# Three reorderings in a gated linear-attention plus mixture-of-experts kernel: the queue of the gate-weight loads, the step in which rows are placed, and the place of decay's exponential

## The chip, the cores and the metric

The kernel runs as one program on one core of a Trainium2 chip. The metric is device time in microseconds, lower is better. A core has a matrix engine (TensorE, PE in the rows; PEld is its weight load), a vector engine (VectorE, DVE), a scalar engine (ScalarE, ACT) that evaluates functions from tables, a general engine (GpSimd, POOL) and an engine that mostly starts transfers (SyncE, SP). ACT, POOL and SP each start DMA transfers from queues of their own. An engine takes its instructions in the order in which they were written, so an instruction that waits holds up everything behind it on its engine.

## The reference, cut to what matters

A recurrent attention with a forget gate, then a mixture of experts in which each token goes to one expert and none is dropped.

```python
# q, k, v, f_logit: (4, 8, 768, 48) float32
f = 1.0 / (1.0 + np.exp(-f_logit))
state = np.zeros((B, H, D, D))
for t in range(S):
    state = f[:, :, t, :, None] * state + np.einsum('bhd,bhe->bhde', k[:, :, t], v[:, :, t])
    y[:, :, t] = np.einsum('bhd,bhde->bhe', q[:, :, t], state)
x = y.transpose(0, 2, 1, 3).reshape(3072, 384)
logits = x @ w_gate                                  # 8 experts
expert_idx = np.argmax(logits, axis=1)
gate_w = softmax(logits)[expert_idx]
for e in range(8):                                   # rows of expert e
    y[rows] = np.maximum(x[rows] @ w1[e], 0.0) @ w2[e]   # 384 -> 1024 -> 384
return gate_w[:, None] * y
```

## The kernel before

**Attention, in twelve units.** The sequence is cut into chunks of 128 tokens; a unit `u` is one chunk of two batches and all eight heads (`NU = 12`). A loop over `n` runs fourteen steps, and step `n` works on several units at once: scores of unit `n`, outputs of unit `n - 1`, and the gate logits and row layout of unit `n - 2`, while the decays of units `n + 1` to `n + 3` are prepared ahead. In this text "step n" begins with the first score matmul of unit `n`, and its start is called S.

**What a unit needs.** `growth` takes the exponential of the forget logit on ACT (L363) and adds one on POOL (L364). `product` is a running product along the sequence on DVE (L371, tile `r`). `by_r` multiplies `k` by `r` on POOL (L383). `log_r` (ACT logarithm, L388) and `decay` (ACT exponential, L394) turn `r` into the decay that `by_decay` multiplies into `q` on DVE (L402). The logarithm and the exponential each need a table load on ACT (`ACT_TABLE_LOAD`). `score` multiplies `q` and `k` on PE (L413) into PSUM tiles `s`, and DVE copies the causal part into `at` with predicated copies (L417), four in a step: two behind the first half of the scores and two behind the second. There are three buffers for `s`, so the second half of the scores needs the first predicated copies done.

**The rest of a step on PE.** `keys` transposes `k` (L426, `kp`; ACT copies the result to `kn`, L431), `rows` multiplies the attention output `ys` of unit `n - 2` by a constant matrix `wx` that holds an identity for laying out rows and the gate weights (L521, `xp`), `within` and `before` make the attention output (L439 and L460, `yt`, copied to `ys` by ACT, L501), `added` makes the state's increment (L476, `dp`), and every second step two small matmuls count the rows by expert (L203 and L204, `rp`). The tiles `kp`, `xp`, `dp` and `rp` share three PSUM buffers in rotation (pool `pst`, tag `tr`), two of `kp`, two of `xp`, one of `dp` and one of `rp` in such a step. So the first `xp` of the next step takes the buffer that `rp` had.

**Routing.** Units are taken in pairs. At the end of an odd step n from 3 to 11, `rows` has finished a pair, `choose` has picked experts (DVE, L191 to L199), `count` has made `rp`, and then `place` and `fill` turn ranks into row numbers: nine small DVE instructions (L210 to L237), which sit on DVE between the state update (L493) and the next step's predicated copies. `sends` then scatters rows of 400 floats to DRAM from POOL (L166), half of a group per step.

**Constants and loads.** `load_consts` starts two transfers from ACT's queue, the mask `mpack` (L152) and the packed constants `fpack` (L153), and behind them four small ones that write the gate weights into the columns of `fpack` that `wx` covers (L157). The last four wait until `fpack` has landed, since they write into it. SP's queue carries the loads of `f`, `k`, `q` and `v` (L356), with the next unit's `f` waiting until an old buffer is free, and the clearing of row regions in DRAM (L323).

**Experts.** Behind the attention come eight experts of three tiles of 128 rows, on PE almost without a gap.

The order of the instructions is written out by hand: what the loop calls first stands first on each engine.

Of the kernel before, what the change touches and what calls it, by code (L numbers as in the profile page):

```python
# [10 lines left out]
F32 = mybir.dt.float32  # L11
# [3 lines left out]
OP = mybir.AluOpType  # L15
AX_X = mybir.AxisListType.X
PSUM = bass.MemoryType.PSUM

B, H, S, D = 4, 8, 768, 48
# [93 lines left out]
def kernel(  # L113
# [22 lines left out]
    def const(name):  # L136
        a, w = fat[name]
        return fpack[:, a : a + w]
# [12 lines left out]
    def load_consts():  # L151
        nc.scalar.dma_start(mpack, nc.inline_tensor(mv, name="c_mpack").ap())  # L152
        nc.scalar.dma_start(fpack, nc.inline_tensor(fv, name="c_fpack").ap())  # L153

        for a, r in halves:
            for b, cols in enumerate((slice(XW, WX), slice(0, E))):
                nc.scalar.dma_start(  # L157
                    wx[r, :, cols],
                    moe_w_gate.rearrange("(p two d) e -> two d p e", two=2, d=D)[a ^ b],
                )  # L160
# [168 lines left out]
    with ExitStack() as st:  # L329
# [56 lines left out]
        def log_r(u, part=whole):  # L386
            x = units[u]
            nc.scalar.activation(x["f"][:, part, 1:CR], x["r"][:, part, 1:CR], AF.Ln)  # L388
# [96 lines left out]
        def update(u):  # L485

            x = units[u]
            new = wk.tile([128, SEG, D], F32, name="state", bufs=4)
            last = _bc(x["last"], 2, D)
            if x["old"] is None:  # L490
                nc.vector.tensor_copy(new, x["dp"])
            else:
                nc.vector.tensor_tensor(new, x["dp"], x["old"], op=OP.add)  # L493
            nc.gpsimd.tensor_tensor(new, new, last, op=OP.mult)
            states[u % 2] = new

        def settle(u):
            x = units[u]
# [6 lines left out]
        def rows(u):  # L505
# [3 lines left out]
            if u == g[0]:  # L509
                n = 2 * len(g)  # L510
                group["xr"] = wk.tile([128, n, ROW], F32, tag="xr", name="xr", bufs=3)
                group["lg"] = wk.tile([128, n, E], F32, tag="lg", name="lg")
                b0 = 2 * (u % 2)
                toks = const("tok").rearrange("p (b c) -> p b c", c=NC)[:, b0 : b0 + n, u // 2]
                nc.gpsimd.tensor_copy(group["xr"][:, :, TOK], toks)
                nc.gpsimd.memset(group["xr"][:, :, USED:ROW], 0.0)
            for a in range(2):
                j = 2 * (u - g[0]) + a
                xp = pst.tile([128, HP, XW], F32, name="xp", **tr)
                for p in range(HP):  # L520
# [4 lines left out]
                        start=True,  # L525
                        stop=True,
                    )
                to = group["xr"][:, j, 0:DM].rearrange("p (h w) -> p h w", h=HP)
                if a:
                    for h in range(2):  # L530
                        nc.scalar.copy(
                            to[:, :, D * h : D * h + D],
                            xp[:, :, XW - D * h - D : XW - D * h],
                        )
                else:
                    nc.scalar.copy(to, xp[:, :, 0 : 2 * D])
                gate = slice(0, E) if a else slice(2 * D, XW)
                nc.vector.reduce_sum(  # L538
                    group["lg"][:, j],
                    xp[:, :, gate].rearrange("p h e -> p e h"),  # L540
                    axis=AX_X,
                )
            if u != g[-1]:
                return None
            return Route(wk, group["lg"], lead["base"], group["xr"], "xs")

        st.enter_context(tc.manual_schedule(engines=ordered))
        ab = (slice(0, HP), slice(HP, SEG))
# [29 lines left out]
        def narrow_early(x, w):  # L578
            narrow(x, w, pst.tile([128, DM], F32, name="yp", **tr), None)

        sends = []
        for n in range(NU + 2):
            here, back, last = n, n - 1, n - 2
            rt = None
# [6 lines left out]
            if n + 1 < NU:  # L591
                by_r(n + 1)
                log_r(n + 1)
            if sends:
                sends.pop(0)()
            if here < NU:
# [8 lines left out]
                    rt.choose()  # L605
            if n + 1 < NU:
                decay(n + 1)
            if n + 3 < NU:
                growth(n + 3)
            if rt:  # L610
# [13 lines left out]
                    by_decay(n + 1, part)  # L624
            if here < NU and here // 2 < NC - 1:
                added(here)
                update(here)
            if rt:
                rt.count(pst.tile([128, 2, rt.n, E], F32, name="rp", **tr))
                rt.place()  # L630
                rt.fill()
                lead["base"] = rt.after
                if n == NU - 3:
                    lack = wk.tile([1, EARLY], F32, name="lack", bufs=1)
                    some = wk.tile([1, 1], F32, name="some", bufs=1)
                    nc.vector.tensor_tensor(
                        lack, rt.after[0:1, 0:EARLY], const("full")[0:1, 0:EARLY], op=OP.is_lt
                    )
                    nc.vector.reduce_max(some, lack, axis=AX_X)
                    nc.vector.tensor_copy(fix, some)  # L640
                if n < NU:
                    for c in range(0, rt.n, 2):
                        sends.append(lambda rt=rt, c=c: rt.send(range(c, c + 2)))
                else:
                    rt.send(range(rt.n))
            if n == NU:
                early_h = early_banks()
                widen(soon[0], weights[0], early_h, range(3))
# [3 lines left out]
                load(n + 4, "f")  # L652
            if n + 3 < NU:
                load(n + 3, "kqv")
            if n < 2:
                for e in range(4 * n, 4 * n + 4):
                    load_pads(e)
# [358 lines left out]
```

## Time and profile before

| What | Value |
|---|---|
| Time, median of 3 runs | 464.23 us (461.31 to 464.49) |
| Profiled execution | 462.27 us, of which span 460.4 us from the first to the last instruction |
| PE busy | 412.5 us (90%), 3580 instructions |
| DVE busy | 168.0 us (36%) |
| ACT busy | 123.3 us (27%) |
| POOL busy | 118.2 us (26%) |
| Moved | 98.33 MB, mean 214 GB/s |

The table is an average over two different halves: some 188 us of attention and routing, in which all engines and the DMA share the work, and some 272 us of experts, which is PE's alone. In the rows, an instruction's idle time in brackets is what its engine waited before it, with the releaser. The granted clock is that of TensorE: 1.00 is 2.4 GHz and 0.50 is 1.2 GHz.

### The profile page before, as it was taken

What the parts mean: (1) busy time and instruction counts of PE and PEld (TensorE: products, weight loads), DVE (VectorE), ACT (ScalarE), POOL (GpSimd) and SP (SyncE); (2) the same over time, 40 slices, a digit from 0 to 9 for tenths busy, and PEclk for the clock granted to TensorE, in tenths of its full rate; (3) what the DMA queues carried; (4) which work ended last, traced back from release to release, by engine and by line L of the source; (5) the groups of instructions that cost most, each with busy time, mean ns of one, the idle gap of its engine ahead of it and who ended that gap; (6) DMA issues with size and microseconds to landing.
All of it is one profiled execution on the core that took longest, in us unless ns stands there. A gap on an engine that the chain in (4) does not pass through costs nothing.

```text
span 460.4 us, 8555 instructions
## 1 busy us (share of the span) xinstructions
PE 412.5 (90%) x3580; PEld 333.1 (72%) x3581; DVE 168.0 (36%) x359; ACT 123.3 (27%) x184; POOL 118.2 (26%) x134
## 2 busy tenths in 40 slices
PE   0178979798979998999999999999999999999992
PEld 0167869697869887777778888857588888777460
DVE  4188895959794554111111211122111111211110
ACT  2677867768674320000000000001000000000010
POOL 6257564748573141000000011000100000000000
PEclk9999997979997999999999999999999999999998
DMA  8999983739981224699992451540079999100000
GB/s 287 348 365 390 390 302 129 263 120 366 338 297 55 76 87 145 220 391 381 393 388 98 154 187 36 183 178 1 31 262 392 395 390 389 38 17 19 18 2 21
DMA packets 42862, 98.33 MB, mean 214 GB/s; under 512 B 3856, under 2 KB 27717, under 8 KB 42816
## 3 DMA queue, kind: packets, MB, share of 16 engines
q1 hardware_dynamic: 38496, 87.48, 52.6%
q0 software_dynamic: 3200, 9.64, 5.5%
q8 instruction: 29, 0.48, 0.4%
q10 hardware_dynamic: 1120, 0.59, 0.4%
q14 instruction: 17, 0.14, 0.1%
HBM read 81.46 MB, written 16.63 MB: 213 GB/s over the span
## 4 chain that ended last, share of the span: by engine, by line
PE 78%; DVE 10%; issue 3%; ACT 3%; DMA 3%; POOL 0%; ACTq 0%; POOLq 0%; DVEq 0%
PE hps L268 26%; PE yps L282 25%; PE s L413 5%; PE xp L521 4%; PE yt L439 3%; PE s L268 2%; PE hps L796 2%; PE yps L824 2%; PE yp L282 2%; DMA fpack<-c_fpack 2%; DVE at L417 2%; PE etp L255 2%; DVE place L225 2%; PE kp L426 2%; DVE r L371 2%
## 5 line engine op out<-in xcount | busy, mean ns | idle before, releaser
L268 PEld LDWEIGHTS hps<-xT,w1t 128*128 128x128 f32 x1056 | 121.1, 192 | 7.3 <-issue 2.3
L268 PE MATMUL hps<-xT,w1t 128*128 128x128 f32 x1056 | 121.8, 275 | 0.0
L282 PE MATMUL yps<-w2t,hT 128*128 128x384 f32 x352 | 117.2, 486 | 0.0
L282 PEld LDWEIGHTS yps<-w2t,hT 128*128 128x128 f32 x352 | 65.2, 190 | 40.8
L166 POOL DMA_INDIRECT out_dram<-ysb,dst x26 | 25.3, 971 | 254.8 <-DVE ysb L289 254.8
L276 ACT ACTIVATE hT<-hps 128x512 f32<-128x512 f32 x22 | 13.1, 597 | 220.0 <-PE hps L268 220.0
L413 PE MATMUL s<-q,k 64*128 64x128 f32 x384 | 34.8, 312 | 36.4 <-POOL last L397 21.7
L413 PEld LDWEIGHTS s<-q,k 64*128 64x128 f32 x384 | 28.7, 210 | 40.2 <-POOL last L397 25.4
L278 DVE TENSOR_SCALAR hT<-hps 128x512 f32<-128x512 f32 x22 | 15.2, 691 | 105.9 <-PE hps L268 105.9
L289 DVE TENSOR_SCALAR ysb<-yps,xrow 128x384 f32<-128x384 f32 x22 | 13.6, 618 | 93.3 <-PE yps L282 93.3
L417 DVE COPY_PREDICATED at<-mpack,s 128x512 f32<-128x512 uint8 x48 | 32.2, 724 | 12.5 <-PE s L413 12.5
L166 POOL DMA_INDIRECT xs<-xr,posi x24 | 27.5, 1147 | 22.9 <-DVE lg L538 8.9
L371 DVE TENSOR_TENSOR_SCAN r<-f,cap 128x1032 f32<-128x1032 f32 (+1 forms) x13 | 28.9, 2225 | 2.3 <-POOL f L364 2.1
L521 PE MATMUL xp<-fpack,ys 128*128 128x104 f32 x192 | 29.4, 317 | 0.2 <-ACT ys L501 0.2
L521 PEld LDWEIGHTS xp<-fpack,ys 128*128 128x128 f32 x192 | 27.2, 226 | 1.7 <-issue 0.4
L383 POOL TENSOR_TENSOR k<-k,r 128x1024 f32<-128x1024 f32 (+1 forms) x13 | 27.1, 2086 | 3.4 <-DVE r L371 3.4
L439 PE MATMUL yt<-at,v 128*64 128x128 f32 x384 | 26.8, 299 | 0.0
L439 PEld LDWEIGHTS yt<-at,v 128*64 128x64 f32 x384 | 23.9, 153 | 1.5 <-issue 0.6
L402 DVE TENSOR_TENSOR q<-q,f 128x512 f32<-128x512 f32 x24 | 17.2, 757 | 21.2 <-ACT f L394 21.2
L397 POOL COPY last<-f 128x8 f32<-128x8 f32 (+1 forms) x13 | 9.9, 768 | 46.1 <-ACT f L394 46.1
L388 ACT ACT_TABLE_LOAD x12 | 15.4, 1283 | 10.9 <-issue 10.7
L364 POOL TENSOR_SCALAR f<-f 128x1032 f32<-128x1032 f32 (+1 forms) x13 | 14.7, 1136 | 3.3 <-ACT f L363 3.3
(109 smaller groups left out, 357.3 us busy)
## 6 DMA issues: line engine op xcount, KB each, us to landing
qw<-in_moe_w_dram SPq DMA_DIRECT2D x16, 1536.0 KB, 12.5
w1t<-in_moe_w_dram SPq DMA_DIRECT2D x8, 1536.0 KB, 9.9
w2t<-in_moe_w_dram SPq DMA_DIRECT2D x8, 1536.0 KB, 13.6
xs<-pad SPq DMA_DIRECT2D x8, 800.0 KB, 11.4
v<-in_vu_dram SPq DMA_DIRECT2D x12, 512.0 KB, 5.6
f<-in_fu_dram SPq DMA_DIRECT2D x11, 516.0 KB, 7.0
k<-in_ku_dram SPq DMA_DIRECT2D x11, 512.0 KB, 7.8
q<-in_qu_dram SPq DMA_DIRECT2D x11, 512.0 KB, 4.9
```

The costliest lines, as they stand in the source:

```text
L166: ins = nc.gpsimd.indirect_dma_start(out=dst, out_offset=bass.IndirectOffsetOnAxis(ap=idx, axis=0), in_=src, in_offset=None, bounds_check= ...
L268: nc.tensor.matmul(hp[g][:, f, :], lhsT=w[0][:, j, b * 128 : b * 128 + 128], rhs=x["xT"][:, j, :], start=j == 0, stop=j == KD - 1,)
L278: nc.vector.tensor_scalar(x["hT"][:, 4:8], hp[1], 0.0, None, op0=OP.max)
L282: nc.tensor.matmul(yp, lhsT=x["hT"][:, f, :], rhs=w[1][:, f, :], start=f == 0, stop=f == NF - 1)
L371: nc.vector.tensor_tensor_scan(x["r"][:, part].rearrange("p s c -> p (s c)"), x["f"][:, part].rearrange("p s c -> p (s c)"), cap[:, part]. ...
L383: nc.gpsimd.tensor_tensor(k, k, r[:, :, 1:CR], op=OP.mult)
L388: nc.scalar.activation(x["f"][:, part, 1:CR], x["r"][:, part, 1:CR], AF.Ln)
L402: nc.vector.tensor_tensor(q, q, x["dec"][:, part], op=OP.mult)
L413: nc.tensor.matmul(ps[h][:, p], lhsT=x["k"][r, s], rhs=x["q"][r, s], start=True, stop=True)
L417: nc.vector.copy_predicated(x["at"][:, a, h], _bc(causal, 1, HP), ps[h])
L439: nc.tensor.matmul(x["yt"][DP * (h ^ a) : DP * (h ^ a) + DP, a, p], lhsT=x["v"][:, a, 2 * p + h], rhs=x["at"][:, a, h, p], start=p == 0, s ...
L521: nc.tensor.matmul(xp[:, p], lhsT=x["ys"][:, a, p], rhs=wx[:, p, 0:XW] if a else wx[:, p, E:WX], start=True, stop=True,)
```

## The change

1. The four gate-weight transfers move from ACT's queue at the start to SP's queue, in step 0 behind the loads of that step and ahead of the clearing of row regions (`load_gate`).
2. `place` and `fill`, which stood at the end of a routing step, move into the following step, behind its first score half, `by_r` and `log_r` (function `settled`). On DVE that is behind the step's first two predicated copies. In the last two steps they stay where they were. The POOL multiply of the state (L494) moves with them, behind the next unit's `by_r`, in every step.
3. The ACT copies of the laid-out rows (L531, L536) leave `rows` and become `lay`, behind `decay`. The DVE reduction of the gate logits (L538) stays and so now stands ahead of those copies.

```diff
@@ load_consts
         nc.scalar.dma_start(fpack, nc.inline_tensor(fv, name="c_fpack").ap())
+    def load_gate():
         for a, r in halves:
             for b, cols in enumerate((slice(XW, WX), slice(0, E))):
-                nc.scalar.dma_start(
+                nc.sync.dma_start(
                     wx[r, :, cols],
...
@@ update
-            nc.gpsimd.tensor_tensor(new, new, last, op=OP.mult)
             states[u % 2] = new
+            return lambda: nc.gpsimd.tensor_tensor(new, new, last, op=OP.mult)
@@ rows -> rows, lay
-                to = group["xr"][:, j, 0:DM].rearrange("p (h w) -> p h w", h=HP)
-                if a:
-                    for h in range(2):
-                        nc.scalar.copy(
...
-                else:
-                    nc.scalar.copy(to, xp[:, :, 0 : 2 * D])
                 nc.vector.reduce_sum(
...
+        def lay(u):
+            x = units[u]
+            for a in range(2):
+                to = x["xr"][:, a, 0:DM].rearrange("p (h w) -> p h w", h=HP)
+                if a:
+                    for h in range(2):
+                        nc.scalar.copy(
...
+                else:
+                    nc.scalar.copy(to, x["xp"][a][:, :, 0 : 2 * D])
+        def settled(n, rt):
+            rt.place()
+            rt.fill()
+            lead["base"] = rt.after
...
+            if n < NU:
+                for c in range(0, rt.n, 2):
+                    sends.append(lambda c=c: rt.send(range(c, c + 2)))
+            else:
+                rt.send(range(rt.n))
@@ the loop
             if n + 1 < NU:
                 by_r(n + 1)
                 log_r(n + 1)
+            if later:
+                settled(*later)
+                later = None
+            if decayed:
+                decayed()
+                decayed = None
             if sends:
                 sends.pop(0)()
...
             if n + 1 < NU:
                 decay(n + 1)
+            if 0 <= last:
+                lay(last)
...
-                update(here)
+                decayed = update(here)
             if rt:
                 rt.count(pst.tile([128, 2, rt.n, E], F32, name="rp", **tr))
-                rt.place()
-                rt.fill()
-                lead["base"] = rt.after
...
+                later = (n, rt)
+                if n >= NU:
+                    settled(*later)
+                    later = None
...
+            if n == 0:
+                load_gate()
```

How the instructions stand is shown at three places. First ACT at the start of the program, before, from the first exponential on (`f` is the forget logit, `r` the running product):

```order
L363 ACTIVATE f<-f 128x516 x2
L152 DMA mpack<-c_mpack 128x128
L153 DMA fpack<-c_fpack 128x1075
L157 DMA fpack<-in_moe_w_gate_dram 48x4x8 x4
L388 ACT_TABLE_LOAD
L388 ACTIVATE f<-r 128x4x128 x2
```

and of the change:

```order
L365 ACTIVATE f<-f 128x516 x2
L152 DMA mpack<-c_mpack 128x128
L153 DMA fpack<-c_fpack 128x1075
L390 ACT_TABLE_LOAD
L390 ACTIVATE f<-r 128x4x128 x2
```

The table load for the first logarithm now stands right behind the start of `fpack`; the four transfers stand on SP behind `v` of unit 3. Second DVE from step 3's `by_decay` to step 4's running product, before (`lg`, `oh`, `ex` are logits, choice and exponents, `rp` the counts, `place` and `posi` row numbers, `su` and `xr` the gate weight):

```order
L402 TENSOR_TENSOR q<-q,f 128x512 x2
L493 TENSOR_TENSOR state<-dp,state 128x384
L210 COPY counts<-fpack 128x8
L211 COPY counts<-rp 128x8x4
L212 SCALAR_TENSOR_TENSOR sums<-fpack,counts 128x40
L222 TENSOR_TENSOR place<-rp,sums 128x32
L225 TENSOR_TENSOR place<-place,oh 128x32
L228 TENSOR_REDUCE posi<-place 128x4
L235 TENSOR_REDUCE su<-ex 128x4
L236 TENSOR_SCALAR su<-su 128x4
L237 RECIPROCAL xr<-su 128x4
L417 COPY_PREDICATED at_97<-mpack,s 128x512 x4
```

and of the change:

```order
L404 TENSOR_TENSOR q<-q,f 128x512 x2
L495 TENSOR_TENSOR state<-dp,state 128x384
L419 COPY_PREDICATED at_97<-mpack,s 128x512 x2
L212 COPY counts<-fpack 128x8
L213 COPY counts<-rp 128x8x4
L214 SCALAR_TENSOR_TENSOR sums<-fpack,counts 128x40
L224 TENSOR_TENSOR place<-rp,sums 128x32
L227 TENSOR_TENSOR place<-place,oh 128x32
L230 TENSOR_REDUCE posi<-place 128x4
L237 TENSOR_REDUCE su<-ex 128x4
L238 TENSOR_SCALAR su<-su 128x4
L239 RECIPROCAL xr<-su 128x4
```

The nine small instructions now stand between the first two and the last two predicated copies. Third ACT in a routing step, before:

```order
L431 COPY kn<-kp 128x512 x2
L536 COPY xr<-xp 128x384
L531 COPY xr<-xp 128x4x48 x2
L394 ACT_TABLE_LOAD
L394 ACTIVATE f<-f 128x8x128
L363 ACTIVATE f<-f 128x1032
L231 ACTIVATE ex<-ex 128x32
```

and of the change:

```order
L433 COPY kn<-kp 128x512 x2
L396 ACT_TABLE_LOAD
L396 ACTIVATE f<-f 128x8x128
L554 COPY xr<-xp 128x384
L549 COPY xr<-xp 128x4x48 x2
L365 ACTIVATE f<-f 128x1032
L233 ACTIVATE ex<-ex 128x32
```

The table load and the exponential of `decay` no longer stand behind the three copies that read `xp`; `growth`'s exponential (L365) still does.

## Rows read from the trace of the kernel before

**Rows 1.** Page, part 2: forty slices of 11.5 us, granted clock in tenths.

```profile
PEclk9999997979997999999999999999999999999998
```

**Rows 2.** Stretches, step by step: length, busy us and instructions by engine, clock, DMA.

```profile
60.80:76.10 15.30, 12.82 (x154) 11.65 (x153) 10.58 (x19) 9.02 (x14) 8.11 (x10) 0.78 0.44 163
76.10:85.80 9.70, 9.70 (x162) 8.73 (x158) 8.06 (x17) 8.32 (x13) 7.36 (x7) 1.00 0.79 271
...
110.80:122.90 12.10, 9.62 (x154) 8.53 (x153) 10.07 (x19) 8.12 (x13) 6.77 (x9) 1.00 0.93 364
...
132.60:147.00 14.40, 11.77 (x122) 10.55 (x121) 8.34 (x21) 6.51 (x9) 6.16 (x9) 0.76 0.35 132
147.00:187.90 40.90, 39.52 (x380) 33.42 (x373) 19.80 (x89) 9.09 (x22) 11.38 (x15) 1.00 0.28 96
187.90:460.40 272.50, 262.34 (x1715) 200.21 (x1713) 44.96 (x95) 15.50 (x26) 24.28 (x25) 0.99 0.53 193
```

**Rows 3.** Timeline of the start: start us, length us, engine, instruction [idle before].

```profile
4.58 0.73 ACTq L153 DMA_DIRECT2D fpack<-c_fpack  x1
4.92 2.81 DVE L371 TENSOR_TENSOR_SCAN r<-f,cap 128x516 f32<-128x516 f32 x2 [0.76 <-POOL f L364]
...
13.62 1.87 ACTq L157 DMA_DIRECT2D fpack<-in_moe_w_gate_dram  x4
...
15.51 1.28 ACT L388 ACT_TABLE_LOAD   x1 [10.69 <-issue]
...
20.77 2.08 PE L413 MATMUL s<-q,k 64*128 64x128 f32 x16 [20.77 <-POOL last L397]
...
25.71 1.06 ACT L388 ACTIVATE f<-r 128x1024 f32<-128x1024 f32 x1 [2.09 <-DVE r L371]
...
32.43 2.08 PE L413 MATMUL s<-q,k 64*128 64x128 f32 x16 [2.11 <-DVE q L402]
```

**Rows 4.** DMA issues at 13.98 and at 44.27 us: size, us to landing.

```profile
f<-in_fu_dram SPq DMA_DIRECT2D x1, 516.0 KB, 4.4
...
f<-in_fu_dram SPq DMA_DIRECT2D x1, 516.0 KB, 11.1
```

**Rows 5.** One stretch, 16 to 58 us: columns as in Rows 2.

```profile
16.00:58.00 42.00, 31.67 (x382) 28.62 (x384) 30.85 (x35) 34.63 (x44) 22.84 (x23) 1.00 1.04 381
```

**Rows 6.** Timeline of step 4, behind the routing of step 3.

```profile
61.05 0.55 DVE L210 COPY counts<-fpack 128x8 f32<-128x8 f32 x1
...
62.33 2.17 POOL L383 TENSOR_TENSOR k<-k,r 128x1024 f32<-128x1024 f32 x1
...
62.74 1.80 DVE L225 TENSOR_TENSOR place<-place,oh 128x32 f32<-128x32 f32 x1
...
65.19 1.31 DVE L417 COPY_PREDICATED at<-mpack,s 128x512 f32<-128x512 uint8 x2
...
65.94 1.16 PE L413 MATMUL s<-q,k 64*128 64x128 f32 x14 [2.48 <-DVE at L417]
```

**Rows 7.** Timeline, the same small instructions at 156 us.

```profile
155.83 0.19 DVE L211 COPY counts<-rp 128x32 f32<-128x32 f32 x1 [1.41 <-PE rp L204]
...
156.57 0.19 DVE L225 TENSOR_TENSOR place<-place,oh 128x32 f32<-128x32 f32 x1
```

**Rows 8.** Stretches of 1 us, PE alone: busy, instructions, granted clock, DMA.

```profile
64.00:65.00 1.00, 0.00 (x0) 1.00 0.88 318
67.00:68.00 1.00, 1.00 (x6) 0.50 0.55 217
```

**Rows 9.** Timeline of step 5, which has no placing in it.

```profile
75.25 1.07 ACT L501 COPY ys<-yt 128x512 f32<-128x512 f32 x2 [0.58 <-PE yt L460]
...
77.38 1.36 DVE L417 COPY_PREDICATED at<-mpack,s 128x512 f32<-128x512 uint8 x2 [0.52 <-PE s L413]
...
78.60 1.06 ACT L431 COPY kn<-kp 128x512 f32<-128x512 f32 x2
...
79.39 2.03 PE L521 MATMUL xp<-fpack,ys 128*128 128x104 f32 x16
```

More of the change, by code (lines that the diff above doesn't have):

```diff
@@ L516, in rows @@
                 nc.gpsimd.memset(group["xr"][:, :, USED:ROW], 0.0)
+            x["xr"], x["xp"] = group["xr"][:, 2 * (u - g[0]) :], []
             for a in range(2):
@@ L527, in rows @@
                     )
-                to = group["xr"][:, j, 0:DM].rearrange("p (h w) -> p h w", h=HP)
-                if a:
-                    for h in range(2):
-                        nc.scalar.copy(
-                            to[:, :, D * h : D * h + D],
-                            xp[:, :, XW - D * h - D : XW - D * h],
-                        )
-                else:
-                    nc.scalar.copy(to, xp[:, :, 0 : 2 * D])
                 gate = slice(0, E) if a else slice(2 * D, XW)
@@ L542, in rows @@
                 )
+                x["xp"].append(xp)
             if u != g[-1]:
@@ L545, in rows @@
             return Route(wk, group["lg"], lead["base"], group["xr"], "xs")
+        def lay(u):
[5 more added lines that the diff above has]
+                        nc.scalar.copy(
+                            to[:, :, D * h : D * h + D],
+                            x["xp"][a][:, :, XW - D * h - D : XW - D * h],
+                        )
+                else:
+                    nc.scalar.copy(to, x["xp"][a][:, :, 0 : 2 * D])
         st.enter_context(tc.manual_schedule(engines=ordered))
@@ L579, in narrow_early @@
             narrow(x, w, pst.tile([128, DM], F32, name="yp", **tr), None)
-        sends = []
+        def settled(n, rt):
+            rt.place()
+            rt.fill()
+            lead["base"] = rt.after
+            if n == NU - 3:
+                lack = wk.tile([1, EARLY], F32, name="lack", bufs=1)
+                some = wk.tile([1, 1], F32, name="some", bufs=1)
+                nc.vector.tensor_tensor(
+                    lack, rt.after[0:1, 0:EARLY], const("full")[0:1, 0:EARLY], op=OP.is_lt
+                )
+                nc.vector.reduce_max(some, lack, axis=AX_X)
+                nc.vector.tensor_copy(fix, some)
+            if n < NU:
[3 more added lines that the diff above has]
+                rt.send(range(rt.n))
+        sends, later, decayed = [], None, None
         for n in range(NU + 2):
@@ L626 @@
                 added(here)
-                update(here)
+                decayed = update(here)
             if rt:
                 rt.count(pst.tile([128, 2, rt.n, E], F32, name="rp", **tr))
-                rt.place()
-                rt.fill()
-                lead["base"] = rt.after
[L633 to L645, printed above, removed]
+                later = (n, rt)
+                if n >= NU:
+                    settled(*later)
+                    later = None
             if n == NU:
```

## The prediction

> **What bounds the kernel now.** The stretches come first: the experts take 272.5 of the 460.4 us and PE is busy in 262.3 of them [rows 2]. The change touches nothing there, so they only move earlier. What is left are 188 us of start and attention. Step by step these split into steps without placing, in which PE has no gap (9.70 us, of which 9.70 busy; the other two such steps, 7 and 9, also take 9.7), and steps that follow a routing step and hold its placing: 15.3, 12.1 and 14.4 us for steps 4, 8 and 10, and step 6 is like step 4 [rows 2]. So PE bounds every second step, and something else costs 2.4 to 5.6 us in the others. The timeline of step 4 names it: PE stands still for 2.48 us ahead of the last 14 of 16 instructions of a score group, released by a predicated copy that starts at 65.19, because DVE has been at the nine small instructions since 61.05 [rows 6].
>
> The clock line comes next: most of the span at 9 tenths or more, with a few slices of 7 [rows 1]. In 64 to 65 us PE does nothing; in 67 to 68 it is busy throughout at a granted clock of 0.50, which is 1.2 GHz [rows 8]. Step 8 has the same 2.48 us of idle PE (12.10 less 9.62) at a clock of 1.00 and takes 12.1 us; steps 4 and 6 take 15.3 at a mean clock of 0.78 [rows 2]. So the same wait costs once or twice: itself, and in three of these four steps some 3.2 us more of half clock.
>
> Last the start. ACT starts the transfer of `fpack` at 4.58, for 0.73 us. It then stands for 10.69 us until its table load at 15.51; within that, at 13.62, it takes 1.87 us to start the four gate loads. The running products that the logarithm needs end at 7.73 (4.92 + 2.81). PE's first score is at 20.77, step 1 at 32.43 [rows 3].
>
> **Change 1, the gate loads: about -6.6 us.** Without them the table load follows at 5.31 and is over by 6.6; the second half of the logarithm waits for 7.73. From the table load to the first score it is 5.26 us now (15.51 to 20.77), so the first score comes between 11 and 14, 7 to 9 us earlier. That doesn't all last. ACT meets `growth` of unit 2 next, whose `f` is started at 13.98 and lands 4.4 us later, at 18.4 [rows 4], and I do not expect it much sooner: the DMA engines are full (381 GB/s, share 1.04) from 16 to 58 us [rows 5]. From 18.4 on ACT needs about 1.0 for that exponential and 1.28 for a table load, so the logarithm of unit 1 starts near 20.7 instead of 25.71: -5.0. In the kernel before, that logarithm waited for a running product and the product of unit 2 was late again behind it; with both early, step 1 starts some 1.6 us sooner still, near 25.8 instead of 32.43. I take -6.6. Bounds: -1.9, if only the issue time goes, and -10.7, the whole idle time. On SP the four loads cost 1.87 us of issue and stand ahead of the clearing of row regions and of `f` of unit 5, all behind a DMA that is full anyhow; `wx` is first read in step 2, more than ten us later. I cost that at nothing; without that cover it is 1.9 us.
>
> The Trainium skill ("DMA: Bandwidth & Descriptors", section "Issuing engines are not separate DMA queues") says that all queues run on the same 16 engines and that another issuing engine saves only the issue time, which is usually small. By that rule the change would be worth the 1.87 us of the four issues. The trace differs: the larger part of the 10.69 us is a wait that stood on ACT's queue for `fpack` to land.
>
> **Change 2, the placing: a wait of 2.48 becomes one of about 0.8.** Let S be a step's start. Step 5 shows where things fall without placing (S = 76.18): the first two predicated copies at S + 1.2 for 1.36, so to S + 2.56, and `xp` at S + 3.2 [rows 9]. With the nine instructions behind those two copies, the second score half no longer waits for them. The next to wait is `xp`: its PSUM buffer is the one that held `rp`, and the last reader of `rp` is the fourth of the nine (L222). With POOL quiet, L211 to the end of L222 take under 0.74 us (155.83 to 156.57) [rows 7], so with the first one about 0.9: `rp` is free at S + 3.5 and PE loses about 0.4. With POOL busy, L225 took 1.80 us rather than 0.19 and ended with POOL's L383 (62.33 + 2.17 = 64.50) [rows 6, 7]. L383 now starts earlier, ahead of the state multiply, so most of it should be over by S + 2.6; if the chain still meets all of it, the wait is 0.4 + 2.2 = 2.6. I take 0.8, nearer to the quiet end. The gap itself falls away, and with it, I expect, the half clock: no step that lost less than 2.4 us shows it.
>
> The Trainium skill ("SBUF — State Buffer", section "SBUF: two separate sides") calls this an exclusive lock between DVE and GpSimd, held for a whole instruction. The 1.80 us above agree. It gives no duration that the sum uses.
>
> **Change 3, decay ahead of the copies: no gain by itself, a wait of 0.6.** It takes the three copies (about 1 us) and their wait for `xp` off the way from logarithm to `by_decay`; in a step without a gap (9.70) nothing waits for that. But the copies now wait for the logit reduction on DVE, behind the running product. That reduction ends near S + 8.5 to S + 9.1 in a step with placing (2.56, the nine at about 1.9 to 2.5, then 1.36, 2.3 and 0.3). Behind it ACT has the copies and `growth` (2.0), then `ys` to the first `kn` (75.25 to 79.1, 3.9) [rows 9]: S + 14.4 to S + 15.0. The second `xp` of the next step needs the `kp` buffer that this `kn` copy frees, at S + 9.9 + 4.2 = S + 14.1. So the steps without placing lose 0.3 to 0.9; I take 0.6.
>
> **The sum.** A step with placing has 9.62 busy us in step 8 [rows 2], of which some 0.5 belong to a score group that is cut in two and counted longer; 9.1 remain, and 9.9 with the new wait of 0.8. Step 4 gets 11.1: `f` of unit 6 is started at 44.27 and lands at 55.4 [rows 4], and a step 4 that begins at 54.2 has ACT waiting for it ahead of `ys` and `kn`. I put 2.0 for that and the 0.8 together (0.4 to 3.5).
>
> - Start to step 4: -6.6.
> - Step 4: 15.3 to 11.1, -4.2. Step 6: 15.3 to 9.9, -5.4. Step 8: 12.1 to 9.9, -2.2. Step 10: 14.4; it has the same wait and half clock as step 6, -5.4.
> - Steps 5, 7, 9: 9.7 to 10.3, +1.8 together.
> - From 147.0 on (40.9 and 272.5): no change. The fifth placing, in step 12, has slack there.
>
> Together -22.0. Against the profiled execution's own 462.27 us this is 440.3, so **440 us**; that execution is 0.4% under the median of 464.23, and the runs differ by 3.2 us, about one stretch of half clock.
>
> **Rivals.**
> - *The half clock stays.* The new waits (0.8 and 0.6, 2.0 in step 4) still make it fall in three steps. For it: the start, and step 4 with its late `f`. Against it: each wait is a third of the old one or less, save in step 4. Price 3 x 3.2 = 9.6: 450 us.
> - *The start gives its gain back.* The loads are full until 58 us [rows 5], so step 4 comes only 1.9 us earlier, by issue time alone. This is also the skill's rule above. Against it: a table load and a logarithm that wait for no load. Price 4.7: 445 us.
> - *The placing only moves its wait.* `xp` waits 2.5 us instead of the scores, with the same half clock. Then only the start and the 1.8 remain: 462.3 - 6.6 + 1.8 = 457.5 us.
> - *Slower.* `xp` waits longer than the scores did, because the chain on DVE meets the growth, `by_r` and state instructions of POOL one behind the other. At 4.4 us in each of five steps (+9.6), with two more half clocks (+6.4) and the start's -6.6, it is 472 us. It decides from a wait of about 3.8 us, where 5 x 1.3 eat up the 6.6. Against it: L383 was the only long one in the way in step 4 [rows 6], and 2.6 is its bound.
>
> **How the numbers follow.** About 1% of the time, 4.6 us, is what a measurement of this kernel can tell from no change. Chances: forecast 0.63, within 436 to 445; half clock stays 0.17; start given back 0.08; placing only moves 0.06; slower 0.03; two of these together and no change 0.03. The bounds of the waits (0.4 to 2.6 in three steps, 0.4 to 3.5 in one) are -2.8 and +6.9, those of the start -4.1 and +4.7, and few of them fall together; 434 to 451 takes in the first three cases. Faster 0.94, same 0.03, slower 0.03.
>
> **What the profile after would show.** ACT's first table load for the logarithm at 5 to 7 us, the first score at 11 to 14 and step 1 at 25 to 27; if step 1 is later than 30, the start failed. No idle PE between the two score halves of steps 4, 6, 8 and 10, a short wait ahead of `xp` in its place, and a second one ahead of the second `xp` of steps 5, 7 and 9. A granted clock of 1.00 through the steps from 4 on. Steps of about 10 us and a tail from step 11 on as long as before. Wrong would be a wait of over 2 us ahead of `xp`, or a clock that falls as often as before.

## The result, and the profile after

The changed kernel took **441.33 us** (median of 4 runs, 440.55 to 441.52) against 463.05 us before: a ratio of 0.953 (95% interval 0.949 to 0.957). On a second occasion, beside the last three experiments, it took 438.45 us (438.00 to 439.31) against 461.46, 0.949 (0.946 to 0.953). The forecast was 440 us. The first profiled execution took 440.55 us with a span of 438.7, 21.7 less than the span before; the working had 22.0 less. The total is nearer than its parts deserve, as the steps show.

The clock line of the page, to be read against [rows 1], has no dip left until the program's end:

```profile
PEclk9999999999999999999999999999999999999997
```

For the start the clock that the rows print says nothing, in either kernel: [rows 5] prints 1.00, but 16 score matmuls take 2.08 us there ([rows 3], and 11.41 below) and 1.16 us later (35.38 below).

Stretches of the first profiled execution, columns as in [rows 2]: steps 4 to 7, step 9, step 10, step 11 to the first experts, and the experts.

```profile
53.74:65.12 11.38, 9.19 (x153) 8.24 (x152) 9.78 (x19) 9.07 (x14) 7.75 (x6) 1.00 0.84 334
65.12:74.91 9.79, 9.79 (x160) 8.83 (x156) 8.12 (x16) 9.33 (x16) 9.31 (x11) 1.00 0.81 286
74.91:84.75 9.84, 9.39 (x153) 8.36 (x153) 9.08 (x20) 6.96 (x11) 7.96 (x8) 1.00 0.73 254
84.75:95.64 10.89, 10.23 (x157) 9.00 (x157) 9.44 (x18) 10.50 (x17) 9.99 (x11) 1.00 1.00 371
...
104.95:115.84 10.89, 10.18 (x156) 8.97 (x156) 9.43 (x18) 9.63 (x16) 9.98 (x11) 1.00 1.01 370
...
115.84:123.93 8.09, 8.09 (x121) 7.22 (x121) 5.88 (x21) 6.78 (x10) 5.54 (x9) 1.00 0.43 154
123.93:166.06 42.13, 40.11 (x375) 33.55 (x371) 19.13 (x88) 9.00 (x22) 10.82 (x15) 1.00 0.27 92
166.06:438.70 272.64, 262.45 (x1715) 200.31 (x1713) 44.94 (x95) 15.51 (x26) 24.35 (x25) 0.99 0.53 193
```

The steps with placing went from 15.3, 15.2, 12.1 and 14.4 us to 11.38, 9.84, 9.31 and 8.09, all at a clock of 1.00. Steps 7 and 9, without placing, went from 9.7 to 10.89. The experts are what they were, 272.6 us.

The start, to be read against [rows 3]:

```profile
6.15 1.28 ACT L390 ACT_TABLE_LOAD   x1 [1.18 <-issue]
...
11.41 2.08 PE L415 MATMUL s<-q,k 64*128 64x128 f32 x16 [11.41 <-POOL last L399]
...
17.76 1.06 ACT L365 ACTIVATE f<-f 128x1032 f32<-128x1032 f32 x1 [5.24 <-DMA f<-in_fu_dram]
...
25.50 0.80 PE L415 MATMUL s<-q,k 64*128 64x128 f32 x4 [1.84 <-DMA k<-in_ku_dram]
...
35.38 1.16 PE L415 MATMUL s<-q,k 64*128 64x128 f32 x16 [1.60 <-DVE q L404]
```

ACT no longer stands 10.69 us ahead of its table load. The first score comes at 11.41 rather than 20.77, then ACT waits 5.24 us for `f` of unit 2. Step 1 starts at 25.50 and step 4 at 53.74, 7.1 us earlier than before. The row of 25.50 names the load of `k`, but `by_r` has worked on that `k` since 19.92; what ends last before it is POOL's copy of `last` (L399, 24.65 to 25.30), so it is the decay chain that releases step 1.

Step 4, to be read against [rows 6]:

```profile
53.45 1.06 ACT L365 ACTIVATE f<-f 128x1032 f32<-128x1032 f32 x1 [1.71 <-DMA f<-in_fu_dram]
...
54.60 1.05 POOL L366 TENSOR_SCALAR f<-f 128x1032 f32<-128x1032 f32 x1 [3.35 <-ACT f L365]
...
55.62 2.18 POOL L385 TENSOR_TENSOR k<-k,r 128x1024 f32<-128x1024 f32 x1
...
56.19 1.64 DVE L212 COPY counts<-fpack 128x8 f32<-128x8 f32 x1
...
58.85 0.20 DVE L224 TENSOR_TENSOR place<-rp,sums 128x32 f32<-128x32 f32 x1
...
59.21 1.00 PE L524 MATMUL xp<-fpack,ys 128*128 128x104 f32 x7 [2.19 <-DVE place L224]
```

The score group is no longer cut in two. PE waits 2.19 us ahead of `xp` instead. The chain is readable: `f` comes 1.71 us late, so POOL's L366 and then `by_r` (L385) are late, and DVE's first small copy, which takes 0.16 us where POOL does not meet it (L210 at 132.86 in the kernel before), takes 1.64 beside `by_r` and ends with it (57.83 and 57.80).

Step 7, where the second `xp` waits for the copy into `kn`:

```profile
89.74 1.14 PE L524 MATMUL xp<-fpack,ys 128*128 128x104 f32 x8 [0.64 <-ACT kn L433]
```

### The profile page after: what moved, and what is told of

It is laid out like the page before. It is cut to its first block, busy times and chain, and to the rows that moved or that the text cites. A ratio compares the mean times of both kernels' runs of the same rounds, so it can differ in the third digit from the quotient of the medians.

```text
span 438.7 us, 8553 instructions
## 1 busy us (share of the span) xinstructions
PE 403.9 (92%) x3580; PEld 324.2 (74%) x3581; DVE 161.7 (37%) x359; ACT 122.7 (28%) x184; POOL 123.4 (28%) x134
## 4 chain that ended last, share of the span: by engine, by line
PE 81%; DVE 6%; DMA 5%; ACT 4%; issue 2%; SPq 0%; POOL 0%; POOLq 0%; DVEq 0%; ACTq 0%
PE hps L270 27%; PE yps L284 26%; PE s L415 4%; DMA k<-in_ku_dram 4%; PE yt L441 3%; PE xp L524 3%; PE s L270 2%; PE hps L822 2%; PE yps L850 2%; PE yp L284 2%; DVE at L419 2%; PE yt L462 2%; PE etp L257 2%; DMA q<-in_qu_dram 2%; DVE r L373 2%
## 5 line engine op out<-in xcount | busy, mean ns | idle before, releaser
L280 DVE TENSOR_SCALAR hT<-hps 128x512 f32<-128x512 f32 x22 | 15.2, 692 | 105.9 <-PE hps L270 105.9
L415 PE MATMUL s<-q,k 64*128 64x128 f32 x384 | 32.6, 307 | 16.0 <-POOL last L399 11.4
L168 POOL DMA_INDIRECT xs<-xr,posi x24 | 34.8, 1450 | 30.0 <-DVE lg L532 10.5
L415 PEld LDWEIGHTS s<-q,k 64*128 64x128 f32 x384 | 27.4, 207 | 19.4 <-POOL last L399 14.7
L419 DVE COPY_PREDICATED at<-mpack,s 128x512 f32<-128x512 uint8 x48 | 32.3, 727 | 16.2 <-PE s L415 12.9
L373 DVE TENSOR_TENSOR_SCAN r<-f,cap 128x1032 f32<-128x1032 f32 (+1 forms) x13 | 29.9, 2305 | 5.3 <-POOL f L366 2.8
L524 PE MATMUL xp<-fpack,ys 128*128 128x104 f32 x192 | 25.0, 281 | 4.0 <-DVE place L224 2.2
L385 POOL TENSOR_TENSOR k<-k,r 128x1024 f32<-128x1024 f32 (+1 forms) x13 | 27.6, 2124 | 1.2 <-DVE r L373 1.2
L524 PEld LDWEIGHTS xp<-fpack,ys 128*128 128x128 f32 x192 | 22.6, 191 | 5.9 <-ACT kn L433 4.7
L441 PE MATMUL yt<-at,v 128*64 128x128 f32 x384 | 23.6, 276 | 0.0
L441 PEld LDWEIGHTS yt<-at,v 128*64 128x64 f32 x384 | 20.7, 137 | 1.2
L366 POOL TENSOR_SCALAR f<-f 128x1032 f32<-128x1032 f32 (+1 forms) x13 | 13.5, 1037 | 14.0 <-ACT f L365 11.8
L404 DVE TENSOR_TENSOR q<-q,f 128x512 f32<-128x512 f32 x24 | 16.2, 717 | 2.7 <-ACT f L396 2.7
L365 ACT ACTIVATE f<-f 128x1032 f32<-128x1032 f32 (+1 forms) x13 | 13.1, 1006 | 9.0 <-DMA f<-in_fu_dram 9.0
```

Source lines behind the costliest of these rows:

```text
L168: ins = nc.gpsimd.indirect_dma_start(out=dst, out_offset=bass.IndirectOffsetOnAxis(ap=idx, axis=0), in_=src, in_offset=None, bounds_check= ...
L280: nc.vector.tensor_scalar(x["hT"][:, 4:8], hp[1], 0.0, None, op0=OP.max)
L373: nc.vector.tensor_tensor_scan(x["r"][:, part].rearrange("p s c -> p (s c)"), x["f"][:, part].rearrange("p s c -> p (s c)"), cap[:, part]. ...
L385: nc.gpsimd.tensor_tensor(k, k, r[:, :, 1:CR], op=OP.mult)
L404: nc.vector.tensor_tensor(q, q, x["dec"][:, part], op=OP.mult)
L415: nc.tensor.matmul(ps[h][:, p], lhsT=x["k"][r, s], rhs=x["q"][r, s], start=True, stop=True)
```

## The experiments

Each set ran beside the kernel before: 461.39, 460.99 and 461.46 us in the three sets. The experts' stretch was 272.6 to 272.7 us in each profile compared across sets here, so lengths of steps may be read across them.

**e1_gate: change 1 alone.**

```diff
-                nc.scalar.dma_start(            # in load_consts
+                nc.sync.dma_start(              # in load_gate, at the end of step 0
```

> The kernel before with change 1 alone (the gate loads on SP at the end of step 0). Theory: ACT's wait for fpack goes, so the first score comes near 11.4 instead of 20.77 and step 4 near 54 instead of 60.9; steps 4, 6, 8 and 10 keep their 2.48 us wait ahead of the second score half. 462.3 - 7 = 455, give or take one stretch of half clock (3.2). Rival (issue time alone): the first score 1.9 us earlier, 460 to 461.

Measured 454.94 us, ratio 0.984 (0.977 to 0.991): 6.4 us less. Step 4 starts at 55.10 instead of 60.87. Two of its steps with placing:

```profile
55.10:67.22 12.12, 9.64 (x154) 8.53 (x153) 10.08 (x19) 8.13 (x13) 6.86 (x9) 1.00 0.73 288
76.93:92.25 15.32, 12.83 (x153) 11.53 (x152) 10.53 (x19) 9.05 (x14) 7.82 (x10) 0.78 0.43 159
```

Both hold the same wait, 2.48 and 2.49 us; only the second is followed by the half clock, for 3.2 us more. The start keeps most of its gain, and issue time alone is ruled out. What it loses is in step 1, which begins 7.3 us earlier (25.17) and takes 11.20 us rather than 9.47; in part its matmuls run at the slow rate of the start for longer (the second score half takes 2.08 us, before 1.16).

**e2_place: change 2 alone** (the hunks `settled`, `later` and `decayed` of the diff). 

> The kernel before with change 2 alone (placing and the state multiply one step later). Theory: first score still at 20.8 and step 4 still at 60.9, but steps 4, 6, 8 and 10 take about 9.9 us each with no wait between the score halves, and the granted clock stays at 1.00: 462.3 - 5.4 - 5.4 - 2.5 - 6.0 = 443. Rival (the wait only moves, with its half clock): 457 to 462. Rival (the half clock is set by something else): 450 to 453, clock near 0.97 as before.

Measured 445.17 us, ratio 0.965 (0.960 to 0.970): 16.2 us less. Step 3, step 4, step 10, and step 11 to the first experts:

```profile
51.28:61.00 9.72, 9.72 (x157) 8.76 (x157) 8.58 (x18) 9.25 (x16) 5.42 (x6) 1.00 0.99 378
...
61.00:71.19 10.19, 9.20 (x153) 8.23 (x153) 8.48 (x19) 8.13 (x13) 6.41 (x6) 1.00 0.60 212
...
119.97:128.99 9.02, 8.16 (x122) 7.26 (x121) 6.23 (x21) 7.43 (x11) 6.02 (x8) 1.00 0.52 187
128.99:169.69 40.70, 39.32 (x370) 33.29 (x371) 20.04 (x89) 8.31 (x21) 11.54 (x15) 1.00 0.28 96
```

Steps 4, 6, 8 and 10 take 10.19, 9.92, 9.70 and 9.02 us at a clock of 1.00, together 18.2 less than before; the span is 18.1 shorter. Ahead of `xp` PE waits 0.99 us in step 4 (forecast 0.8) and not at all in the other three. But the starts of two steps show a wait that the forecast didn't know:

```profile
90.83 1.16 PE L413 MATMUL s<-q,k 64*128 64x128 f32 x16 [0.51 <-issue]
...
128.99 1.16 PE L413 MATMUL s<-q,k 64*128 64x128 f32 x16 [0.86 <-issue]
```

The scores of steps 7 and 11 begin right after the first half of `by_decay` on DVE (which starts at 90.05 and 128.19 and takes 0.64 us): with the placing out of the way, PE is early enough to wait for `q`.

**e3_lay: change 3 alone** (the hunks `rows -> rows, lay` of the diff). 

> The kernel before with change 3 alone (decay's exponential ahead of the copies of x). Theory: nothing to gain, since in no step does PE wait for decay; the second xp of steps 5, 7 and 9 may wait up to 0.6 us for kn: 462 to 464. Rival (decay's place carried part of the gain): the steps from 4 on get shorter, 455 to 459.

Measured 461.30 us, ratio 1.000 (0.997 to 1.003). Nothing by itself, as expected, though as a sum: step 2 takes 8.22 us instead of 9.25, step 3 takes 10.52 instead of 9.72 (the second `xp` waits 0.56 us for `kn`), and the half clock stands in steps 4, 6 and 8 instead of 4, 6 and 10 (step 10 waits 2.57 us and stays at 1.00). That in no step PE waits for decay was wrong already for the kernel before, whose steps 2 and 3 begin behind such waits:

```profile
41.90 1.16 PE L413 MATMUL s<-q,k 64*128 64x128 f32 x16 [1.60 <-DVE q L402]
...
51.15 1.16 PE L413 MATMUL s<-q,k 64*128 64x128 f32 x16 [0.95 <-POOL last L397]
```

**f_fill: PE works in the wait.** The kernel before, with work that it does not need:

```diff
                 keys(here)
+                if here in (4, 6, 8, 10):
+                    for _ in range(2):       # the eight transposes of k, into the same kp
+                        for a in range(2):
+                            for p in range(HP):
+                                nc.tensor.transpose(units[here]["kp"][a][:, p], ...
                 keep(here)
```

> The kernel before, with the eight transposes of k repeated twice into the same tiles in steps 4, 6, 8 and 10, so that PE works some 2.1 of the 2.48 us in which it stood still ahead of the second score half. Nothing else is changed; the repeats are work that the kernel does not need. Theory (PE's standing still is what brings the half clock): clock 1.00 in all steps, 3 x 3.2 us gone, 453, up to 457 if kn and what is behind it come later by the repeats. Rival (the half clock comes from load or from the time, whatever PE does in the wait): three stretches at 0.50 as before, 462 to 465.

Measured 453.50 us, ratio 0.982 (0.977 to 0.986): 16 matmuls more in each of four steps, and 7.9 us less.

```profile
20.68:61.56 40.88, 33.81 (x453) 30.45 (x453) 32.64 (x44) 32.87 (x43) 21.83 (x24) 0.87 1.01 370
61.56:73.69 12.13, 11.38 (x170) 10.27 (x169) 10.10 (x19) 8.25 (x13) 6.87 (x9) 1.00 0.54 205
83.40:95.54 12.14, 11.39 (x170) 10.28 (x169) 10.11 (x19) 8.25 (x13) 6.74 (x9) 1.00 0.58 198
105.25:117.39 12.14, 11.38 (x170) 10.27 (x169) 10.10 (x19) 8.25 (x13) 6.76 (x9) 1.00 0.89 351
127.11:139.23 12.12, 10.38 (x138) 9.28 (x137) 8.04 (x21) 7.34 (x11) 6.05 (x8) 1.00 0.37 136
```

The first row is the start of this execution up to step 4, the others are steps 4, 6, 8 and 10. PE's idle time ahead of the second score half falls from 2.48 to 0.75 us (0.89 in step 10), and each step takes 12.1 us at 1.00: the length that the wait gives without the half clock. Of the twelve such waits (2.4 to 3.3 us) in the profiles of the kernel before, e1_gate and e3_lay nine were followed by the half clock, of these four none. So the half clock does come from PE's standing still, and the 3.2 us that went with it are a cost of the wait. The start of this execution takes 0.8 us more than in the kernel before (40.88 against 40.10), which takes back part of the 9.6. Its 0.87 can't be set against the 1.00 of [rows 5], which leaves out the slow matmuls of the start.

**l3_nolay: changes 1 and 2 without 3.** 

> Changes 1 and 2 without change 3 (the copies of x stay ahead of decay). Theory: changes 1 and 2 add up, 6.4 and 16.2 us less than before, so 1.5 to 3 us less than the changed kernel: about 439, with steps 5, 7 and 9 at 9.72 instead of 9.79, 10.89 and 10.89, no wait ahead of the second xp, and the stretch from step 11 to the experts at 40.7 instead of 42.1. Rival (change 3 pays once the other two are in, since the steps are then short enough to wait for decay): 2 us or more above the changed kernel, 443 to 446. Rival (the 1.4 us of the tail are no matter of change 3): the tail stays at 42.1, about 440.5.

Measured 440.04 us, ratio 0.959 (0.952 to 0.966). The two changes nearly add up: 6.4 and 16.2 make 22.6, and 21.0 is measured. Steps 5, 7 and 9 are at 9.7 as expected. What it gains there it loses elsewhere: step 2 has a half clock (10.61 us), and step 10 takes 10.42. The row behind the latter:

```profile
113.16 3.51 DVE L404 TENSOR_TENSOR q<-q,f 128x512 f32<-128x512 f32 x2
...
113.93 2.18 POOL L385 TENSOR_TENSOR k<-k,r 128x1024 f32<-128x1024 f32 x1
```

`by_decay` takes 1.28 us elsewhere (83.97 in the changed kernel, for one); here its second half stands until `by_r` on POOL is over. The expectation of 1.5 to 3 us under the changed kernel is not borne out: on its second occasion the changed kernel is even 1.6 us lower, though the intervals of the two ratios overlap.

**gate_act: the gate loads on ACT's queue, late.**

```diff
-                nc.sync.dma_start(
+                nc.scalar.dma_start(            # still at the end of step 0
```

> The changed kernel with the four gate loads back on ACT's queue, but at the end of step 0 in the order of the program. Theory (what counted was that ACT stood behind a wait for fpack, not which queue carries the loads): fpack has long landed there, so only the issue time returns, 0 to 1.9 us: 441.3 to 443.2, first score near 11.4. Rival (the queue is what counts): the start's gain is lost, first score near 20, 447 to 448.

Measured 438.89 us (438.66 to 440.15), the first score at 11.30. What counted is the place in ACT's order, not the queue.

**state_back: the POOL multiply of the state at its old place.**

```diff
-                decayed = update(here)
+                update(here)()
```

> The changed kernel with the POOL multiply of the state back behind the state update at the end of a step, so that by_r comes 0.8 us later on POOL and more of it stands beside the placing on DVE. Theory (the small DVE instructions are stretched where they stand beside by_r on POOL): the wait ahead of xp grows in steps 6, 8 and 10 from 0 to 0.2 us to about 1, +1 to +3: 442.5 to 444.5. Rival (the placing has slack there, or the stretch does not depend on POOL): 441 to 442, waits as in the changed kernel.

Measured 439.53 us (439.36 to 440.15), between the two occasions of the changed kernel: no loss is shown, and the expectation for steps 6, 8 and 10 was wrong. DVE is held longer, as expected (L212 takes 1.15 us in step 6 against 0.91), but nobody waits for it:

```profile
78.36 1.15 DVE L212 COPY counts<-sums 128x8 f32<-128x8 f32 x1
79.11 2.03 PE L524 MATMUL xp<-fpack,ys 128*128 128x104 f32 x16
...
79.91 0.21 DVE L224 TENSOR_TENSOR place<-rp,sums 128x32 f32<-128x32 f32 x1
```

`xp` starts 0.80 us ahead of L224, the last reader of `rp`. So it isn't `rp`'s buffer that it takes here. The waits written into the changed program say the same, the first `xp` of steps 4 and 6, and `dp` of step 6:

```
124 L524 MATMUL xp_672<-fpack_58,ys_602 128x104 [waits DVE_49,Activation_49]
182 L524 MATMUL xp_973<-fpack_58,ys_903 128x104 [waits Activation_49]
188 L478 MATMUL dp_1028<-v_600,kn_942 64x48 [waits DMAHW6_49,DVE_49]
```

In step 4 alone the first `xp` waits for DVE; in step 6 (and 8 and 10) it waits for ACT only, and in 6 and 8 `dp`, some 5 us later, is what stands behind DVE. The sentence ahead of the prediction that gives `rp`'s buffer to the next step's first `xp` is right for the kernel before: its program puts the two into the same PSUM bank in steps 4, 6, 8 and 10 (7, 5, 6 and 7). In the changed program, and in that of e2_place, they share a bank in step 4 alone (7); in the other three `rp` has bank 5 and `xp` bank 7. So the change itself, its second part, moved the buffers. In step 4, where `xp` does stand behind `rp`'s readers, state_back waits longer, 2.42 us, and takes 13.20 us at 0.87.

**pads_late: changes 1 and 2, the clearing of row regions spread.**

```diff
-            if n < 2:
-                for e in range(4 * n, 4 * n + 4):
+            if n < 3:
+                for e in range(3 * n, min(3 * n + 3, E)):
                     load_pads(e)
```

> Changes 1 and 2 without change 3, and the clearing of the row regions spread over steps 0 to 2 (three, three, two) instead of 0 and 1 (four, four), so that the loads of f, k, q and v of the next units stand ahead of it. Theory (step 4 is late because f of unit 6 is late on a full DMA): steps 3 and 4 get shorter by 0.5 to 2 us together, 437 to 438.5. Rival (the same bytes have to pass by step 4 anyhow, or the scatter of step 4 then waits for the clearing): no change against the kernel without change 3, or 1 to 2 us more.

Measured 439.44 us against 440.04 without the spreading, 0.6 less and within their scatter (439.09 to 443.57, 439.34 to 444.07). Step 4 takes 10.20 us in both, and in neither does ACT wait for `f` there, so the theory has nothing to show; that step 4 begins at 53.52 rather than 55.33 is in good part the half clock in step 2 of the other. For the rival there is a row: the scatter of step 4 stands until 62.84,

```profile
62.84 1.69 POOL L168 DMA_INDIRECT xs<-xr,posi  x1 [5.53 <-DVE lg L540]
```

(that reduction had long ended, so it was another, and the profile doesn't say which; in the other kernel the wait is 2.91 us), and behind it POOL is late, so that step 5 takes 10.87 us instead of 9.71.

**after_again.** 

> The changed kernel once more, beside the next three. Open is whether the 1.4 us that it lost between step 11 and the first experts (42.1 us against 40.7 in every other kernel) belong to it or to that one execution. If they belong to the kernel: 441 to 441.5, that stretch 42.1 again. If to the execution: 439.5 to 440, that stretch 40.7.

Measured 438.45 us. The stretch from step 11 to the experts is 40.71:

```profile
53.00:65.74 12.74, 10.81 (x154) 9.77 (x153) 9.93 (x19) 10.57 (x16) 8.47 (x10) 0.87 0.85 337
104.66:115.25 10.59, 9.96 (x156) 8.83 (x156) 9.41 (x18) 10.15 (x17) 9.69 (x11) 1.00 0.99 368
115.25:123.34 8.09, 8.09 (x121) 7.22 (x121) 5.92 (x21) 6.17 (x9) 5.74 (x9) 1.00 0.48 173
123.34:164.05 40.71, 39.33 (x374) 33.31 (x371) 19.28 (x88) 9.10 (x22) 10.88 (x15) 1.00 0.28 96
```

So the 1.4 us of the tail belong to the first profiled execution, not to the order of the instructions. In step 4 the wait ahead of `xp` is 1.93 us and this time the half clock follows it (12.74 at 0.87, against 11.38 at 1.00), for 1.6 us more of busy PE.

**log_late: the logarithm behind the copies of `kn`.**

```diff
                 by_r(n + 1)
-                log_r(n + 1)
...
                 keep(here)
+            if n + 1 < NU:
+                log_r(n + 1)
```

> The changed kernel with the logarithm called behind the copies of kn, so that on ACT kn stands ahead of a table load and the logarithm. Theory (in steps 7 and 9 the second xp waits 0.64 us for kn, which frees its PSUM buffer, because ACT comes to kn late): those waits go and nothing else changes, since ACT has the same work to do before decay: 1 to 2 us less than the changed kernel, 439.3 to 440.3. Rival (decay then comes later, and by_decay with it): the waits go, but the next scores wait for q instead, 441 to 444.

Measured 444.72 us (443.19 to 446.25), 6.3 more than the changed kernel beside it. The rival was right, and more than that. The waits of `xp` in steps 7 and 9 are gone; the scores of steps 7 and 9 wait 0.85 us at their start; and in step 9 a choice on DVE meets `by_r`:

```profile
113.99 2.74 DVE L194 TENSOR_TENSOR eq<-lg,mx 128x32 f32<-128x32 f32 x1
...
114.48 2.19 POOL L385 TENSOR_TENSOR k<-k,r 128x1024 f32<-128x1024 f32 x1
...
117.54 0.61 PE L205 MATMUL rp<-oh,fpack 128*128 128x32 f32 x2 [2.61 <-DVE ex L201]
```

An instruction of 0.19 us ends at 116.73, when `by_r` ends (116.67), and PE loses 2.61 us. Behind that wait the half clock falls, so that step 10 takes 10.49 us at 0.75 instead of 8.09. The page "SBUF — State Buffer" of the Trainium skill (section "SBUF: two separate sides") says that DVE instructions of certain kinds, those with two inputs in SBUF among them, and GpSimd share a pair of ports, which whoever starts first keeps for the whole instruction. That DVE is held until `by_r` is over agrees (2.74 against 0.19 us, and 3.51 against 1.28 above); that the first to start keeps the ports isn't shown, since here the record of the DVE instruction starts first (113.99 against 114.48).

**mix1 and mix2.** In mix1 the copies of `x` are late in steps 2 and 3 alone, and the state's multiply is back; mix2 is mix1 with the spread clearing of pads_late.

```diff
-            if 0 <= last:
-                lay(last)
+            if 0 <= last < 2:        # from unit 2 on, lay stands in rows again
+                lay(last)
...
-                decayed = update(here)
+                update(here)()
```

> The changed kernel with two edits: the copies of x stand behind decay in steps 2 and 3 alone and ahead of it from step 4 on (as in the kernel before), and the POOL multiply of the state stands at the end of its step again. Theory (change 3 helps steps 2 and 3, where the scores wait for decay, and costs steps 5, 7 and 9, where xp then waits for kn; and by_r on POOL, when it may start early, stretches by_decay on DVE): step 4 starts near 53.5, steps 5, 7 and 9 take 9.7, no by_decay of 3.5 us, the tail 40.7: 437.5 to 438.5. Rival (the two orders only shift the same waits): 439 to 441.

> The kernel mix1 with the clearing of the row regions spread over steps 0 to 2. Theory (f of unit 6 is late in step 4 because the clearing stands ahead of it): step 4 takes 10.2 instead of about 11.2, some 1 us less than mix1: 436.5 to 437.5. Rival (the scatters of step 4 then hold POOL until the clearing has landed, as in pads_late, and step 5 gives it back): the same as mix1, within 0.5.

mix1 took 439.33 us (437.70 to 440.14), no better than the changed kernel at 438.45 and in the range of the rival. Steps 5, 7 and 9 are 9.7 as meant, but its profiled start lost more to the half clock (step 1 takes 11.20 us, step 2 9.54, against 9.65 and 8.22 in mix2), and step 4 starts at 56.86. mix2 took **436.99 us** (436.64 to 437.46), 1.5 us under the changed kernel beside it with no overlap of the runs; ratio to before 0.946 (0.943 to 0.950). It is the fastest kernel of the study.

```profile
53.52:63.75 10.23, 9.19 (x153) 8.23 (x153) 8.41 (x19) 7.80 (x12) 8.18 (x9) 1.00 1.00 386
63.75:73.47 9.72, 9.72 (x161) 8.76 (x157) 8.42 (x18) 9.14 (x15) 9.25 (x9) 1.00 0.76 269
```

Step 4 takes 10.23 us and step 5 gives nothing back: mix2's step 4 starts at 53.52, where the changed kernel's does (53.00 and 53.74), but its ACT does not wait for `f` there. mix1's step 4 is just as short, after a later start, so what of mix2's gain each edit gives isn't separated. That `f` comes earlier with the clearing spread is shown, though. Where it is not spread and step 4 starts at 53.0 to 53.7 (the changed kernel twice, gate_act, state_back), ACT gets `f` at 53.05 to 54.20 after waits of 1.7 to 2.5 us; with it spread ACT takes `f` at 51.90 (pads_late) and 51.52 (mix2) without a wait.

## Why the prediction was right, and where not

- **Start: right.** Forecast 6.6 us, measured 7.1 to step 4 in place and 5.8 alone. Each point of the chain (table load 6.15, first score 11.41, `f` of unit 2 at 17.76, step 1 at 25.50) came within 0.7 us of its forecast or inside its range. gate_act adds that the queue itself is nothing. On SP the four loads took 4.13 us rather than 1.87, and the first `xp` (38.83) didn't wait for them, as costed.
- **The wait between the score halves and its half clock: right.** e2_place has neither from step 4 on, and f_fill shows that the one brings the other. The statement that no step that lost less than 2.4 us shows the half clock is refuted: after_again has it behind 1.93 us. In the changed kernel only step 4 waits that long, and there the rival that the half clock stays did come in, in one of two profiled executions.
- **Step 4: right in sum (11.1 against 11.38), by another path.** The working had 0.8 for `xp` and 1.2 for ACT's wait for `f` ahead of `ys` and `kn`, 2.0 together. PE waits once, 2.19 us ahead of `xp`, since late `f` pushed `by_r` onto the chain of the placing; without late `f` the wait is 1.00 in l3_nolay and 1.04 in mix2. A wait of over 2 us ahead of `xp` was named as a sign of being wrong: it came, in this step alone.
- **Steps 6, 8 and 10: right result for a wrong reason.** 9.9 was forecast with a wait of 0.8 in it. There is no wait for `rp`: the step that failed is that `xp` takes its buffer, which was carried over from the kernel before and which the changed program keeps in step 4 only. Step 8 (9.31) and step 10 (8.09) came out shorter.
- **Change 3: the term that failed.** "Nothing waits for that" was read from steps that had no gap in the kernel before, and not from its steps 1 to 3, which begin behind 2.11, 1.60 and 0.95 us of it ([rows 3] and the rows under e3_lay). Once the placing is gone PE does wait for `q` (e2_place, 0.51 and 0.86 us), so an earlier decay pays: step 10 takes 8.09 with it and 9.02 without (e2_place, mix2), step 2 8.23 and 9.25 (pads_late). Against it stands what was forecast, the second `xp` behind `kn` (0.64 us in steps 7 and 9, none in 5), and those two steps cost 0.9 (second occasion) to 1.2 each, not 0.6. The two sides nearly cancel, which is why the sum didn't notice: alone it is 461.30 against 461.39.
- **The tail: forecast 0, measured +1.4 the first time and 0 the second.** In the first profiled execution ACT and DVE both start 1.3 to 1.5 us late near 125 us (`ys` at 125.57, the predicated copy at 126.39), with the same instructions as in the second. The cause stays open.

The errors are -0.5 at the start, +0.3 in step 4, +0.6 in steps 5, 7 and 9, -1.5 in steps 8 and 10, and +1.4 in the tail: +0.3 together. Steps 6 and 10 were costed from 15.3 and 14.4 by one mechanism; that step 10 lacks the state's increment and could fall to 8.09 was not seen. So the mechanisms of the two large terms were right, and that the sum is off by only 0.3 is luck.

## What to carry to other kernels

Look at what stands behind a waiting instruction on its engine before asking what the transfer costs: four small loads held ACT's next 10 us, and moving them later on the same queue cured it as well. Read which buffer a tile takes, and so whom it waits for, from the program's own waits, in every step and of the changed program: the tile that came behind the readers of `rp` was `xp` in all four steps before, and `dp` in steps 6 and 8 behind the change. And a step that shows no gap says nothing about what its engine will wait for once the gaps around it are gone.

## What the runs showed that was not expected

- A wait of PE of 2.4 to 2.5 us was followed by the half clock in some steps and not in others of the same execution (e1_gate: 12.12 us at 1.00 in step 4, 15.32 at 0.78 in step 6, behind 2.48 and 2.49 us); what decides is not shown. It cost 3.1 to 3.2 us in steps 4 and 6 of the kernel before and 1.6 in step 4 of after_again. In steps 4 to 10 it followed waits from 1.93 us up, not all of them (2.57 in e3_lay), and none of 1.69 us (log_late, step 4) or less.
- Extra matmuls made a kernel 7.9 us faster (f_fill).
- Which DVE instruction meets `by_r` on POOL decides more than how much of DVE is busy: beside the same POOL instruction, the stretched DVE instruction held nobody up in step 6 of state_back and PE for 2.6 us in step 9 of log_late.
